# Transposing queries and keys on the DMA crossbar in place of TensorE, in an attention and MLP-mixer kernel

## The chip, the cores and the metric

The kernel runs on one core of one Trainium2 chip. The metric is the device time of one launch in microseconds (us); lower is better. A ratio is worked out from runs of both kernels in the same rounds on the same chip; it is not quite the ratio of the medians that are quoted beside it.

## The reference

Eight batches, eight heads, 576 tokens, head size 64. Block-causal attention (blocks of 64) is followed by an MLP mixer: a token mix with width 256 and a channel mix with width 1536, both with residuals.

```python
# q, k, v: (8, 8, 576, 64), drawn as randn * 0.1
scores = (1 / np.sqrt(64)) * q @ k.transpose(0, 1, 3, 2)
scores = np.where(block_i >= block_j, scores, -1e9)      # blocks of 64
attn = softmax(scores)
x = (attn @ v).transpose(0, 2, 1, 3).reshape(8, 576, 512)
h = relu(x.transpose(0, 2, 1) @ w_tok1) @ w_tok2         # 576 -> 256 -> 576
u = x + h.transpose(0, 2, 1)
out = u + relu(u @ w_ch1) @ w_ch2                        # 512 -> 1536 -> 512
```

## The kernel before

Heads are worked on in pairs, four pairs per batch, 32 in all (pair 0 to pair 31). GpSimd (POOL) issues the loads into SBUF, the on-chip memory, which also cast to bf16; queries and keys arrive there with tokens on the partitions (the 128 rows of that memory). The score matmul needs the head dimension on the partitions, so both must be transposed: five 128x128 blocks per tensor and pair, on TensorE into PSUM, the memory that its results go to, and copied from there. The keys of the two heads go into two tiles whose other half stays zero, so each score matmul spans all 128 partitions.

```python
def attention_pair(b, hp, x_sb, preloaded=None):
    qraw, kraw = preloaded if preloaded is not None else load_qk_pair(b, hp)

    qT_ps = ps_tr.tile([128, SP], BF16, name="trp")
    for c in range(NS):                                   # NS = 5, SP = 640
        nc.tensor.transpose(qT_ps[:, 128 * c : 128 * (c + 1)], qraw[:, c], ident)
    qT = qkT_p.tile([128, SP], BF16, name="qT")
    nc.vector.tensor_copy(qT, qT_ps)
    kT_ps = ...                                           # the same for kraw
    kTh = [r_kta.next(), r_ktb.next()]
    nc.vector.tensor_copy(kTh[0][0:64, :], kT_ps[0:64, :])
    nc.scalar.copy(kTh[1][64:128, :], kT_ps[64:128, :])

    for hh in range(2):
        # ... load v1; score matmuls into PSUM tiles sc[0..3]
        # ... ScalarE: exp(sc) -> e[0..3];  VectorE: four masks (memset) on e
        # ... value matmuls, into a free part of sc[3]
        nc.vector.reciprocal(rinv, u_view[:, :, 64:65])
        nc.vector.tensor_tensor(out=x_sb[...], in0=u_view[...], in1=rinv[...], op=MULT)
        # ... and a second tensor_tensor for the last 64 tokens
```

The pairs of batch b are traced between the parts of the mixer of batch b-1. A list scheduler then fixes each engine's instruction order when the program is built. At run time every engine works strictly in that order.

```python
for b in range(B + 1):
    attention_pair(b, 0, x_sb)
    pu_sb = token_mix(px)                  # of batch b-1, and so on
    p_uT = transpose_u(pu_sb)
    channel_gT(p_uT, p_gT, 0, 4)
    attention_pair(b, 1, x_sb)
    channel_gT(p_uT, p_gT, 4, 8)
    attention_pair(b, 2, x_sb)
    channel_gT(p_uT, p_gT, 8, 12)
    attention_pair(b, 3, x_sb)
    channel_h2_out(pb, p_gT, pu_sb)        # stores 1.15 MB on SP's DMA queue
```

The softmax here doesn't subtract the row's maximum and nothing guards it: scores larger than these inputs give would overflow.

## Time and profile before

| | before |
|---|---|
| median time | 415.43 us (2 runs, 415.31 to 415.54) |
| span in the profile | 412.9 us |
| first token-mix matmul of batch 1's mixer | 99.90 us |
| from one batch's first token-mix matmul to the next one's | 46.23 us, five times, then 45.67 |
| from the last of these boundaries (376.71) to the end | 36.2 us |

The first token-mix matmul of each batch is the clock that this document uses: its start times are read off the TensorE timeline. The mixer of batch 0 (its first one is at 41.38 us) runs beside pairs 4 to 7 and belongs to the start. From here on, "the first boundary" is that of batch 1's mixer, "a batch" is the stretch from one boundary to the next (the first of them holds pairs 8 to 11), and "a late batch" is one of the last of these.

Two lines of the page of before matter beyond those that the prediction shows: busy time by engine, and the queue that SP feeds (packets, MB, share of 16 engines). The third, from a table of stretches, is one exact batch (columns: length, busy time of PE, PEld, DVE, ACT, POOL with counts, granted clock, DMA share, GB/s).

```profile
PE 368.6 (89%) x3194; PEld 229.3 (56%) x3232; DVE 175.8 (43%) x674; ACT 221.4 (54%) x507; POOL 261.0 (63%) x403
...
q1 hardware_dynamic: 4864, 9.44, 6.3%
```

### The profile page before, as it was taken

To read this page: it belongs to the slowest core of one execution; us is meant where nothing else is said; L and a number is where in the kernel's file an instruction comes from. 1 tells how busy PE (TensorE), PEld (TensorE's weight loads), DVE (VectorE), ACT (ScalarE), POOL (GpSimd) and SP (SyncE) were. 2 spreads that over 40 slices of the span, in tenths; PEclk is the share of its full clock that TensorE was granted. 3 is DMA by queue.
4 is the path that set the end of the run, shared out by engine and by line. 5 is a ranking of instruction groups with operands and counts; after the bars stand their busy time and mean duration, and the time that the engine had idled before them with its cause. 6 is when DMAs were issued, how large, how long until landed. Compare 5 with 4: busy or idle time off the path is not lost.

```text
span 412.9 us, 8622 instructions
## 1 busy us (share of the span) xinstructions
PE 368.6 (89%) x3194; PEld 229.3 (56%) x3232; DVE 175.8 (43%) x674; ACT 221.4 (54%) x507; POOL 261.0 (63%) x403
## 2 busy tenths in 40 slices
PE   1676659999999999999999999999999999999996
PEld 1454247754676456744666457744666457744752
DVE  2244324543545364543554363543555363534112
ACT  9635037742677058742687058732687068730830
POOL 9999389999999775983679375973679320000000
PEclk9998859999999999999999999999999999999999
DMA  6999999999988894785668494885658550003003
GB/s 40 103 60 111 206 78 58 59 60 152 74 58 57 52 156 31 51 54 128 42 41 54 33 154 30 52 52 129 44 38 51 51 110 0 2 2 114 2 2 114
DMA packets 124730, 27.91 MB, mean 68 GB/s; under 512 B 117200, under 2 KB 119568, under 8 KB 124688
## 3 DMA queue, kind: packets, MB, share of 16 engines
q0 software_dynamic: 119824, 17.92, 60.2%
q1 hardware_dynamic: 4864, 9.44, 6.3%
q8 instruction: 26, 0.43, 0.4%
q14 instruction: 16, 0.13, 0.1%
HBM read 35.78 MB, written 9.44 MB: 110 GB/s over the span
## 4 chain that ended last, share of the span: by engine, by line
PE 52%; ACT 22%; POOL 9%; DVE 8%; DMA 5%; issue 3%; ACTq 0%; POOLq 0%
PE mps L336 22%; PE mps L319 18%; ACT e L224 6%; ACT e L223 5%; ACT kTb L195 5%; DMA wc_sb<-in_moe_w_ch_dram 4%; PE sc L238 4%; ACT e L225 3%; PE sc L214 3%; DVE u_sb L290 3%; POOL qraw L116 2%; POOL v L202 2%; ACT uT L306 2%; DVE qT L188 1%; ACT gT L326 1%
## 5 line engine op out<-in xcount | busy, mean ns | idle before, releaser
L319 PE MATMUL mps<-uT,wc_sb 128*128 128x288 bf16 x768 | 111.6, 286 | 1.0
L336 PE MATMUL mps<-wc_sb,gT 128*128 128x512 bf16 x464 | 110.8, 379 | 0.8
L319 PEld LDWEIGHTS <-wc_sb 128*128 128x128 bf16 x768 | 71.0, 97 | 28.4 <-issue 10.6
L116 POOL DMA_DIRECT2D qraw<-in_q_dram x64 | 55.3, 864 | 43.8 <-PE trp L192 28.8
L326 ACT ACTIVATE gT<-mps 128x288 bf16<-128x288 f32 x144 | 59.0, 410 | 28.1 <-PE mps L319 20.7
L336 PEld LDWEIGHTS <-gT 128*128 128x128 bf16 x480 | 44.5, 98 | 50.8 <-issue 5.1
L195 ACT COPY kTb<-trp 64x640 bf16<-64x640 bf16 x32 | 22.0, 687 | 89.5 <-DVE kTa L194 89.1
L202 POOL DMA_DIRECT2D v<-in_v_dram x64 | 56.3, 880 | 21.4 <-PE sc L214 18.5
L116 POOL DMA_DIRECT2D kraw<-in_k_dram x64 | 56.5, 883 | 7.0 <-PE trp L192 5.2
L343 DVE TENSOR_TENSOR o_sb<-mps,u_sb 128x512 f32<-128x512 f32 (+1 forms) x40 | 27.6, 690 | 71.3 <-PE mps L336 71.3
L238 PEld LDWEIGHTS <-e 128*128 128x128 bf16 x960 | 41.6, 101 | 16.9 <-issue 6.9
L214 PE MATMUL sc<-qT,kTb 128*128 128x64 bf16 (+4 forms) x190 | 43.7, 292 | 2.9 <-issue 0.4
L122 POOL DMA_DIRECT2D kraw<-in_k_dram x64 | 42.3, 660 | 1.0 <-DMA wc_sb<-in_moe_w_ch_dram 1.0
L122 POOL DMA_DIRECT2D qraw<-in_q_dram x64 | 40.9, 640 | 2.7 <-DMA wc_sb<-in_moe_w_ch_dram 2.7
L238 PE MATMUL sc<-v,e 128*128 128x65 bf16 x900 | 41.7, 195 | 1.1 <-ACT e L226 0.8
L206 POOL DMA_DIRECT2D v<-in_v_dram x64 | 41.4, 647 | 0.4 <-PE sc L214 0.3
L225 ACT ACTIVATE e<-sc 128x512 bf16<-128x512 f32 x60 | 36.0, 600 | 3.3 <-PE sc L214 1.5
L224 ACT ACTIVATE e<-sc 128x512 bf16<-128x512 f32 x60 | 35.7, 595 | 3.7 <-PE sc L214 3.7
L223 ACT ACTIVATE e<-sc 128x512 bf16<-128x512 f32 x60 | 35.8, 597 | 3.4 <-PE mps L238 1.9
L306 ACT COPY uT<-trp 128x512 bf16<-128x512 bf16 (+1 forms) x36 | 19.5, 544 | 29.9 <-PE trp L301 28.8
L326 DVE TENSOR_SCALAR gT<-mps 128x288 bf16<-128x288 f32 x48 | 22.0, 458 | 26.1 <-PE mps L319 25.6
L214 PE MATMUL sc<-qT,kTa 128*128 128x64 bf16 (+4 forms) x162 | 27.8, 280 | 4.3 <-ACT e L223 2.6
(61 smaller groups left out, 367.9 us busy)
## 6 DMA issues: line engine op xcount, KB each, us to landing
out_dram<-o_sb SPq DMA_DIRECT2D x8, 1024.0 KB, 4.3
qraw<-in_q_dram POOLq DMA_DIRECT2D x64, 64.0 KB, 2.8
kraw<-in_k_dram POOLq DMA_DIRECT2D x64, 64.0 KB, 2.7
v<-in_v_dram POOLq DMA_DIRECT2D x64, 64.0 KB, 2.8
wc_sb<-in_moe_w_ch_dram POOLq DMA_DIRECT2D x4, 384.0 KB, 6.8
wc_sb<-in_moe_w_ch_dram POOLq DMA_DIRECT2D x6, 256.0 KB, 11.9
qraw<-in_q_dram POOLq DMA_DIRECT2D x64, 8.0 KB, 2.3
kraw<-in_k_dram POOLq DMA_DIRECT2D x64, 8.0 KB, 2.3
```

What stands on the lines that cost most here:

```text
L116: nc.gpsimd.dma_start(out=t[:, c0:c1, hh, :], in_=src[b, 2 * hp + hh, 128 * c0 : 128 * c1, :].rearrange("(c p) d -> p c d", p=128),)
L122: nc.gpsimd.dma_start(out=t[0:64, 4, hh, :], in_=src[b, 2 * hp + hh, 512:576, :])
L195: nc.scalar.copy(kTh[1][64:128, :], kT_ps[64:128, :])
L202: nc.gpsimd.dma_start(out=v1[:, 0:4, 0:64], in_=v[b, h, 0:512, :].rearrange("(c p) d -> p c d", p=128),)
L214: nc.tensor.matmul(out=sc[tix][:, c0 : c0 + wdt], lhsT=kT[:, j0 : j0 + 128], rhs=qT[:, ist : ist + wdt], start=True, stop=True,)
L223: nc.scalar.activation(e[0], sc[0], EXP, scale=scale)
L224: nc.scalar.activation(e[1][:, 0:512], sc[1], EXP, scale=scale)
L225: nc.scalar.activation(e[2][:, 0:512], sc[2], EXP, scale=scale)
L238: nc.tensor.matmul(out=u_view[:, I, 0:65], lhsT=exp_lhsT(e, I, J), rhs=v1[:, J, 0:65], start=(J == 0), stop=(J == I),)
L319: nc.tensor.matmul(out=g_ps[:, 0:288], lhsT=wc1_sb[:, m, 128 * cc : 128 * (cc + 1)], rhs=uT[:, m, 288 * sh : 288 * (sh + 1)], start=(m == ...
L326: nc.any.tensor_scalar_max(gT[:, cc, 288 * sh : 288 * (sh + 1)], g_ps[:, 0:288], 0.0)
L336: nc.tensor.matmul(out=h2_ps, lhsT=gT[:, cc, 128 * si : 128 * (si + 1)], rhs=wc2_sb[:, cc, :], start=(cc == 0), stop=(cc == NDC - 1),)
```

## The change

The intent is to take the transposes of queries and keys off TensorE, the bound. The DMA crossbar does them from SBUF to SBUF, one instruction per tensor and pair, issued from SP. The query copy and the PSUM tiles go with them; both key copies move to VectorE.

```diff
-        qT_ps = ps_tr.tile([128, SP], BF16, name="trp")
-        for c in range(NS):
-            nc.tensor.transpose(qT_ps[:, 128 * c : 128 * (c + 1)], qraw[:, c], ident)
-        qT = qkT_p.tile([128, SP], BF16, name="qT")
-        nc.vector.tensor_copy(qT, qT_ps)
-        (the same for kT_ps, from kraw)
+        qT = qkT_p.tile([128, NS, 128], BF16, name="qT")
+        nc.sync.dma_start_transpose(
+            out=qT, in_=qraw.rearrange("p c h d -> p (c h d)")
+        )
+        qT = qT.rearrange("p c s -> p (c s)")
+        (the same for kTr, from kraw)
         kTh = [r_kta.next(), r_ktb.next()]
-        nc.vector.tensor_copy(kTh[0][0:64, :], kT_ps[0:64, :])
-        nc.scalar.copy(kTh[1][64:128, :], kT_ps[64:128, :])
+        nc.vector.tensor_copy(kTh[0][0:64, :], kTr[0:64, :])
+        nc.vector.tensor_copy(kTh[1][64:128, :], kTr[64:128, :])
```

More of the change, by code (lines that the diff above doesn't have):

```diff
@@ L182, in attention_pair @@
         qraw, kraw = preloaded if preloaded is not None else load_qk_pair(b, hp)
-        qT_ps = ps_tr.tile([128, SP], BF16, name="trp")
-        for c in range(NS):
-            nc.tensor.transpose(qT_ps[:, 128 * c : 128 * (c + 1)], qraw[:, c], ident)
-        qT = qkT_p.tile([128, SP], BF16, name="qT")
-        nc.vector.tensor_copy(qT, qT_ps)
-        kT_ps = ps_tr.tile([128, SP], BF16, name="trp")
-        for c in range(NS):
-            nc.tensor.transpose(kT_ps[:, 128 * c : 128 * (c + 1)], kraw[:, c], ident)
+        qT = qkT_p.tile([128, NS, 128], BF16, name="qT")
[3 more added lines that the diff above has]
+        qT = qT.rearrange("p c s -> p (c s)")
+        kTr = qkT_p.tile([128, NS, 128], BF16, name="kTr")
+        nc.sync.dma_start_transpose(
+            out=kTr, in_=kraw.rearrange("p c h d -> p (c h d)")
+        )
+        kTr = kTr.rearrange("p c s -> p (c s)")
         kTh = [r_kta.next(), r_ktb.next()]
-        nc.vector.tensor_copy(kTh[0][0:64, :], kT_ps[0:64, :])
-        nc.scalar.copy(kTh[1][64:128, :], kT_ps[64:128, :])
+        nc.vector.tensor_copy(kTh[0][0:64, :], kTr[0:64, :])
+        nc.vector.tensor_copy(kTh[1][64:128, :], kTr[64:128, :])
         for hh in range(2):
```

## The prediction

> **What bounds the kernel now.** I read the page's 40 slices first, then a table of stretches, one per batch, then the TensorE timeline at a batch boundary, and last the waits. The slices:
>
> ```profile
> PE   1676659999999999999999999999999999999996
> PEclk9998859999999999999999999999999999999999
> DMA  6999999999988894785668494885658550003003
> ```
>
> TensorE (PE) is full from slice 7 on, at full granted clock; before that it is not, while DMA is. So there are two regimes. The stretches (columns: length, busy time and instruction count of PE, PEld, DVE, ACT, POOL, then granted clock, DMA share, GB/s):
>
> ```profile
> 0.00:53.30 53.30, 29.58 (x225) 17.52 (x228) 17.07 (x92) 25.98 (x68) 44.63 (x74) 0.93 0.99 106
> 53.30:99.50 46.20, 42.50 (x385) 27.79 (x388) 18.97 (x78) 24.37 (x55) 45.57 (x71) 0.90 0.92 62
> 192.00:238.20 46.20, 44.24 (x403) 27.59 (x406) 21.98 (x82) 26.33 (x59) 31.52 (x48) 1.00 0.69 65
> 330.70:376.90 46.20, 44.23 (x400) 27.50 (x402) 21.96 (x82) 26.33 (x59) 2.65 (x4) 1.00 0.13 30
> ```
>
> A steady batch takes 46.2 us, with PE busy 44.2, ACT 26.3, DVE 22.0. In the last of them DMA has nearly stopped (0.13) and the period is the same: data movement doesn't set it, TensorE does. In the first two stretches POOL, which issues all loads, is busy 44.6 and 45.6 us: the start is paced by load issue. What the change removes stands in the timeline at a batch boundary (start, length, engine, line, operation):
>
> ```profile
> 145.57 0.44 PE L186 MATMUL trp<-ident,qraw 128*128 128x128 bf16 x5
> 145.85 0.44 PE L192 MATMUL trp<-ident,kraw 128*128 128x128 bf16 x5
> 146.13 1.24 PE L266 MATMUL mps<-x_sb,w_sb 128*128 128x512 bf16 x4
> ```
>
> The next group starts 0.28 us after each group of five: a pair of tensors really occupies 0.56 us of TensorE, not 10 x 219 ns. The waits tell where loads hold TensorE (us, times, longest), and how long the ring makes the loads wait for the transposes:
>
> ```profile
> PE trp L186 <- DMA qraw<-in_q_dram: 13.5, 3, 6.8
> PEld L186 <- DMA qraw<-in_q_dram: 7.2, 1, 7.2
> PE trp L192 <- DMA kraw<-in_k_dram: 5.0, 7, 1.9
> POOL qraw L116 <- PE trp L192: 28.8, 8, 8.4
> ```
>
> The first three all fall before about 62 us; later the loads are ahead and wait for room.
>
> **What the Trainium skill says.** (1) "VectorE: DVE Perf Modes", The three transpose paths: 390 ns for a 128x128 bf16 transpose on TensorE, 1309 ns on the DMA crossbar. Our trace has 219 ns for one record and 56 ns as spacing in a run of five, so the page's figure is that of one alone; I take 56. (2) "DMA: Bandwidth & Descriptors", Latency and other measured facts: an effective 261 GB/s for the DMA transpose in one kernel, 350 to 400 when contiguous. One instruction here moves 128 x 640 x 2 B = 164 KB, an estimate of 0.63 us at 261 GB/s. (1) read literally for five blocks in a row gives 6.5 us. The two differ tenfold, and no transpose is in the trace of before; this is the main uncertainty. (3) The same page, DMA Transpose (X-bar) and SWDGE vs HWDGE vs iDMA: this transpose is issued from SP or ACT only, and its descriptors are generated in hardware. So it doesn't lengthen POOL's issue queue, and SP has little else: in the waits it sat 384.6 us waiting for output tiles. (4) "SBUF — State Buffer", SBUF: two separate sides: a fast VectorE copy within SBUF and GpSimd's descriptor writing lock each other out. The new key copies are of that kind; before, their source was PSUM. Each lasts well under a POOL issue (0.77 us), so I give it at most 1 us in the whole kernel.
>
> **The change part by part.**
> TensorE loses 64 groups of five transposes: 64 x 0.28 = 17.9 us. Not all of it counts. Pairs 0 to 3 run before 53 us, where TensorE waits for loads anyway: 0. Pairs 4 to 7 (the stretch 53.3 to 99.5) are still paced by POOL, at 1.3 us per load and its tail, six loads per pair, 7.8 us per pair, against score groups 7.6 us apart in the chain: I count 0.5 us of their 2.24. Batches 2 to 7 (pairs 8 to 31) are TensorE's: 24 x 0.56 = 13.4 us. Sum: 13.9 us.
> VectorE loses the query copy (486 ns) and the PSUM form of the key copy (476 ns) and gains two 64x640 copies from SBUF. The trace has no such copy; I guess 0.25 us each. Net -0.46 us of 5.5 us per pair: off the path. ScalarE loses 687 ns per pair. That copy stands on the chain with 4.5% of the span, but the chain follows releasers: in steady batches TensorE had work from the mixer meanwhile. The direct TensorE waits there sum to 1.2 us per batch, 0.2 of them for scores behind the exponential. I count nothing.
> The crossbar gains 64 instructions, 8 per batch: 8 x 0.63 = 5 us of 46.2. The DMA share of 0.69 then becomes 0.80. I take issue to landing as 3.3 us, an estimate: in this trace a 128 KB output store lands in 2.9 us, plus some queueing. In steady state that is hidden. The query buffer of pair p is free after the scores of pair p-4, loads are at least two pairs ahead (20 us), and a transpose needs neither the PE order nor the PSUM slots.
> At the start it is not hidden. Pair 2's scores began at 28.07 and pair 3's at 35.50, just after their keys had landed; each comes some 3 us later. The stall before pair 4 absorbs that, 6.78 us of TensorE idle before 55.23. In the changed instruction order the transposes of u and 22 channel matmuls (2.7 us) stand ahead of pair 4's scores, so TensorE works there while the crossbar does; then pairs 5 to 7 are again load plus 3.3 us. I count +1.5 us for the start.
> Moved work: comparing instruction orders, the scheduler brings the second pair of a batch forward into the token-mix section, where before there was one pair. In that section ScalarE must do four heads of exponentials (4 x 1.65 = 6.6 us, at 0.5 us spacing), one ReLU 0.6 and four uT copies 2.4: 9.6 us, against some 10 us of TensorE work (scores 2.7, values 1.9, token mix 4.3, transposes 1.2). That is nearly a tie, in order on both sides, so I charge 0.4 us per batch of extra stalls: 6 x 0.4 = 2.4 us.
> Sum: 415.4 - 13.9 + 1.5 + 2.4 = 405.4. Greedy scheduling may equally fill holes that existed (about 2 us of idle PE per batch), so I shade it down a little: 404 us.
>
> **The rivals.**
> The crossbar is slow. At 6.5 us per instruction the SP queue needs 8 x 6.5 = 52 us per batch, above 46.2: it becomes the bound, and the kernel goes to 64 x 6.5 = 419 plus about 40 of start and tail, some 455 us. For it: the page's 1309 ns, and small DMA packets here are slow (119824 packets take 60.2% of 16 engines for 412.9 us, 33 ns each). Against it: the 261 GB/s, and at 33 ns each the 640 rows of 256 B cost only 640 x 33 / 16 = 1.3 us. In between, at 2 to 3 us, a batch needs 16 to 24 us beside about 32 us of present DMA time: a near tie, 410 to 425 us. I give 12% to clearly slow and 10% to the middle.
> The gain is eaten by waits. The crowded section becomes ScalarE's, or VectorE, in order, stalls at a key copy whose transpose is late and holds back the masks and normalisation behind it. Then the period stays near 46 and the time is 410 to 416 us. For it: ACT 9.6 against PE 10. Against: ACT is busy only 26.3 of 46.2 us over a batch, and the DVE copies come long after the transposes.
> The full gain. Nothing is lost at the boundary and the start is neutral: 415.4 - 13.9, less about 3 us of holes filled, 398 us.
>
> **Range and chances.** The 2% line is 407.1 us. Between the full gain (398) and gain eaten (415) I see 404 as middle, with the line inside the spread, and a tail above it from a slow crossbar. Low 397, high 424. Faster by over 2%: 0.57; within: 0.27; slower: 0.16.
>
> **What would show it.** Right: no trp from qraw or kraw; steady stretches of about 44.2 us; crossbar landings near 3 us and a DMA share near 0.8; TensorE rows without waits on VectorE's key copies after 100 us. Wrong in the crossbar: landings of 6 us and more, DMA share near 1 in every stretch, VectorE waiting for transposes in steady batches, the period above 48. Wrong in the boundary: the same landings, but PE idle behind ACT between the token mix and the first channel matmuls, period at 46. Wrong in the start: the first batch's end moves by more than 3 us from 99.5.

## More of the kernel before

```profile
284.82:331.04 46.22, 44.25 (x402) 27.63 (x405) 21.97 (x83) 26.33 (x59) 31.52 (x48) 1.00 0.69 65
```

TensorE is busy 44.25 of 46.22 us, so 1.97 us per batch are idle. SP's queue carries the output stores only.

## The result, and the profile after

The changed kernel takes 410.19 us (median of 2 runs, 409.72 to 410.66). The ratio to before is 0.988, 95% interval 0.984 to 0.992: some 1.2% faster, less than half of what was predicted. Its profile has a span of 408.9 us.

The slices of the page after:

```profile
PE   0254079999749689999999999999999999999996
...
PEclk9966559999959899999999999999999999999999
DMA  7999999999999999989999999778629341003003
```

The same four stretches as in the prediction, then, in the fifth and sixth row, two exact batches (columns as above):

```profile
0.00:53.30 53.30, 14.33 (x130) 9.01 (x132) 10.41 (x72) 19.69 (x57) 43.41 (x71) 0.76 1.12 116
53.30:99.50 46.20, 42.75 (x379) 26.41 (x381) 23.40 (x96) 25.68 (x63) 43.89 (x67) 0.91 1.24 108
192.00:238.20 46.20, 45.59 (x393) 27.85 (x396) 22.73 (x89) 25.21 (x61) 45.41 (x70) 1.00 1.25 117
330.70:376.90 46.20, 45.28 (x377) 27.42 (x381) 19.14 (x75) 24.72 (x59) 2.62 (x4) 1.00 0.19 51
104.76:162.98 58.22, 45.66 (x363) 27.78 (x366) 22.37 (x85) 24.29 (x59) 55.21 (x85) 0.88 1.23 113
289.45:331.47 42.02, 41.57 (x362) 25.85 (x365) 19.62 (x80) 24.11 (x59) 10.54 (x16) 1.00 0.53 59
```

(The DMA share adds up the times of all packets. It can pass 1, as in four of these rows, when packets of one engine overlap.) Two things contradict each other at first sight. Late in the kernel a batch takes 42.02 us, 4.2 us less than before, with TensorE busy 41.57. But one batch, 104.76 to 162.98, takes 58.22 us, for nearly the same number of matmuls. The start suffered too: in the first 53 us TensorE is busy 14.33 us, where it was 29.58. The start times of the first token-mix matmuls give the whole account:

| stretch | before, us | after, us | difference |
|---|---|---|---|
| start to first boundary | 99.90 | 104.76 | +4.9 |
| first batch after it | 46.23 | 58.22 | +12.0 |
| next five batches, sum | 230.58 | 209.73 | -20.9 |
| last boundary to end | 36.2 | 36.2 | 0.0 |
| span | 412.9 | 408.9 | -4.0 |

The TensorE timeline at a late boundary (start, length, engine, line, operation) has no transposes of queries or keys any more, and scores stand between the token-mix matmuls:

```profile
288.80 0.82 PE L215 MATMUL sc<-qT,kTa 128*128 128x512 bf16 x5
289.45 0.38 PE L267 MATMUL mps<-x_sb,w_sb 128*128 128x512 bf16 x1
289.86 0.19 PE L215 MATMUL sc<-qT,kTa 128*128 128x64 bf16 x1
290.10 0.38 PE L267 MATMUL mps<-x_sb,w_sb 128*128 128x512 bf16 x1
```

The waits after (engine, tile and line, what it waited for: us, times, longest):

```profile
DVE kTa L195 <- DMA kTr<-kraw: 53.4, 11, 11.4
...
PE mps L215 <- DVE kTa L195: 37.1, 4, 13.6
...
PE sc L215 <- DVE x_sb L255: 7.5, 1, 7.5
...
PE sc L239 <- DVE e L231: 3.2, 1, 3.2
```

VectorE (DVE) now waits 53.4 us for transposed keys, in only 11 places. TensorE waits 37.1 us for key copies in the start (L215 with `mps`, the first batch's even heads), and 7.5 us once for VectorE's normalisation of `x_sb`. That last wait is in the long batch, and the two timelines around it show what happened. VectorE first:

```profile
107.75 0.21 DVE L255 TENSOR_TENSOR x_sb<-sc,rinv 64x64 bf16<-64x64 f32 x1
108.02 0.09 DVE L233 MEMSET e<- 64x32 uint32 x1
108.06 0.09 DVE L234 MEMSET e<- 64x32 uint32 x1
115.83 0.32 DVE L195 COPY kTa<-kTr 64x640 bf16<-64x640 bf16 x1 [7.68 <-DMA kTr<-kraw]
116.07 0.18 DVE L248 RECIPROCAL rinv<-sc 128x5 f32<-128x5 f32 x1
...
116.94 0.42 DVE L249 TENSOR_TENSOR x_sb<-sc,rinv 128x256 bf16<-128x256 f32 x1
117.28 0.20 DVE L255 TENSOR_TENSOR x_sb<-sc,rinv 64x64 bf16<-64x64 f32 x1
```

and TensorE in the same time:

```profile
109.44 0.60 PE L215 MATMUL sc<-qT,kTa 128*128 128x512 bf16 x3
117.54 0.66 PE L215 MATMUL sc<-qT,kTa 128*128 128x320 bf16 x3 [7.51 <-DVE x_sb L255]
```

VectorE stands 7.68 us at a key copy (L195) whose transpose hasn't landed. Behind that copy, in VectorE's order, stands the normalisation of another pair (pair 8, second head), whose value matmuls TensorE had finished at about 108.7. It reads `sc`, and TensorE's next scores, of pair 9, need that PSUM buffer. So TensorE stops too, for 7.51 us. The keys at which VectorE waited belong to pair 10, whose own scores are far from due (they begin at 133.52); nothing but the order made them urgent. The 3.2 us wait in the list above is a second stall of the kind, in the same batch: VectorE stood 5.93 us at the keys of pair 13, until 137.85, with masks for TensorE's next value matmuls behind them. SP's timeline shows when the transpose of pair 10's keys was issued:

```profile
104.98 1.20 SPq L185 DMA_TRANSPOSE qT<-qraw  x1
106.69 0.41 SPq L347 DMA_DIRECT2D out_dram<-o_sb  x1
107.23 0.56 SPq L351 DMA_DIRECT2D out_dram<-o_sb  x1
108.18 3.00 SPq L190 DMA_TRANSPOSE kTr<-kraw  x1
```

It was issued 1 us behind the output store of batch 0, and it landed 7.6 us after its issue, about twice the median. But it couldn't have been issued much earlier: the last load of these keys had landed at 108.03. VectorE came to the copy at 108.15 (115.83 less 7.68), before the transpose was even issued, so a landing of the usual length would have stopped it as well, for less long. The queue and issue lines give that median (last column):

```profile
q1 hardware_dynamic: 47872, 19.93, 24.5%
...
qT<-qraw SPq DMA_TRANSPOSE x32, 3.8
kTr<-kraw SPq DMA_TRANSPOSE x32, 3.6
```

The crossbar's share of the queue is 24.5% less the stores' 6.3% of before, 18.2% of 16 engines' 408.9 us: 74.4 us, or 1.16 us of packet time per transpose (an estimate, as the stores are taken to cost what they did before).

### The profile page after: what moved, and what is told of

The parts are those of the page before. It is cut to its first block, busy times and chain, and to the rows that moved or that the text cites. A ratio compares the mean times of both kernels' runs of the same rounds, so it can differ in the third digit from the quotient of the medians.

```text
span 408.9 us, 8119 instructions
## 1 busy us (share of the span) xinstructions
PE 346.4 (85%) x2881; PEld 212.9 (52%) x2912; DVE 162.4 (40%) x653; ACT 203.3 (50%) x496; POOL 262.0 (64%) x403
## 3 DMA queue, kind: packets, MB, share of 16 engines
q1 hardware_dynamic: 47872, 19.93, 24.5%
## 4 chain that ended last, share of the span: by engine, by line
PE 73%; DMA 12%; POOL 6%; issue 3%; DVE 3%; ACT 2%; POOLq 0%; ACTq 0%; SPq 0%; DVEq 0%
PE mps L337 24%; PE mps L320 21%; PE sc L215 10%; PE sc L239 7%; DMA kTr<-kraw 6%; DMA v<-in_v_dram 5%; PE mps L267 4%; PE mps L284 4%; PE trp L302 2%; POOL kraw L116 1%; POOL qraw L116 1%; DMA kraw<-in_k_dram 1%; POOL kraw L122 1%; POOL qraw L122 1%; ACT e L224 1%
## 5 line engine op out<-in xcount | busy, mean ns | idle before, releaser
L320 PE MATMUL mps<-uT,wc_sb 128*128 128x288 bf16 x768 | 108.0, 287 | 0.4
L203 POOL DMA_DIRECT2D v<-in_v_dram x64 | 58.6, 916 | 46.1 <-PE sc L215 33.2
L327 ACT ACTIVATE gT<-mps 128x288 bf16<-128x288 f32 x167 | 68.4, 411 | 23.4 <-PE mps L320 12.8
L116 POOL DMA_DIRECT2D qraw<-in_q_dram x64 | 61.5, 968 | 17.1 <-DMA qT<-qraw 7.6
L116 POOL DMA_DIRECT2D kraw<-in_k_dram x64 | 62.4, 978 | 4.3 <-issue 2.5
L122 POOL DMA_DIRECT2D kraw<-in_k_dram x64 | 47.1, 736 | 2.0 <-DMA wc_sb<-in_moe_w_ch_dram 1.1
L215 PEld LDWEIGHTS <-kTa 128*128 128x128 bf16 x192 | 16.7, 102 | 59.4 <-DVE kTa L195 25.3
L122 POOL DMA_DIRECT2D qraw<-in_q_dram x64 | 46.6, 727 | 1.6 <-DMA wc_sb<-in_moe_w_ch_dram 1.6
L207 POOL DMA_DIRECT2D v<-in_v_dram x64 | 43.4, 678 | 1.6 <-DMA w_sb<-in_moe_w_tok_dram 1.6
L215 PE MATMUL sc<-qT,kTb 128*128 128x64 bf16 (+3 forms) x191 | 43.3, 294 | 0.6 <-DMA kraw<-in_k_dram 0.2
L215 PE MATMUL mps<-qT,kTa 128*128 128x64 bf16 (+4 forms) x24 | 6.6, 416 | 37.1 <-DVE kTa L195 37.1
L215 PE MATMUL sc<-qT,kTa 128*128 128x512 bf16 (+1 forms) x168 | 28.5, 279 | 9.0 <-DVE x_sb L255 7.5
L195 DVE COPY kTa<-kTr 64x640 bf16<-64x640 bf16 x32 | 12.3, 385 | 56.8 <-DMA kTr<-kraw 53.4
```

The costliest lines, as they stand in the source:

```text
L116: nc.gpsimd.dma_start(out=t[:, c0:c1, hh, :], in_=src[b, 2 * hp + hh, 128 * c0 : 128 * c1, :].rearrange("(c p) d -> p c d", p=128),)
L122: nc.gpsimd.dma_start(out=t[0:64, 4, hh, :], in_=src[b, 2 * hp + hh, 512:576, :])
L203: nc.gpsimd.dma_start(out=v1[:, 0:4, 0:64], in_=v[b, h, 0:512, :].rearrange("(c p) d -> p c d", p=128),)
L207: nc.gpsimd.dma_start(out=v1[0:64, 4, 0:64], in_=v[b, h, 512:576, :])
L215: nc.tensor.matmul(out=sc[tix][:, c0 : c0 + wdt], lhsT=kT[:, j0 : j0 + 128], rhs=qT[:, ist : ist + wdt], start=True, stop=True,)
L320: nc.tensor.matmul(out=g_ps[:, 0:288], lhsT=wc1_sb[:, m, 128 * cc : 128 * (cc + 1)], rhs=uT[:, m, 288 * sh : 288 * (sh + 1)], start=(m == ...
```

## The experiments

Twelve kernels ran, eleven of them to explain the time. Ratios are to the kernel before in the same rounds (its medians there: 414.41, 414.99 and 414.63 us).

**No transposes at all** (a wrong result):

```diff
-        (the two crossbar transposes and the two key copies)
+        qT = r_qt.next()                       # fixed tiles, set to zero once
+        kTh = [r_kta.next(), r_ktb.next()]
```

> No transposes at all: queries and keys are fixed zero tiles, the result is wrong on purpose; loads, exponentials and the rest stay. This is what the change could win at most. Theory A (the changed kernel loses its gain in the loaded first 160 us, to keys that land late): steady batches of 42 us as in the changed kernel, a start as in the kernel before, so 415.4 - 6 x 4.2 - 1 = about 389 us. Rival (the 42 us of the changed kernel come from data being further ahead, not from TensorE's work): steady batches of 44 us, about 401 us.

Measured: 401.87 us, ratio 0.969 (0.967 to 0.971). It isn't the clean bound that it was meant to be: nothing reads the loaded queries and keys any more, so the loads come in another order and the values come late. TensorE's waits:

```profile
PE sc L227 <- DMA v<-in_v_dram: 25.7, 11, 10.5
```

One batch, 177.25 to 235.02, takes 57.8 us. So the total is near the rival's 401 us by accident, as late batches aren't at its 44 us. What can be used is the late batch: 41.9 us (280.73 to 322.62), 0.1 less than with the crossbar. The crossbar doesn't hold up a late batch. A side finding: this kernel passes the correctness check. With inputs of 0.1 the attention is nearly uniform, and zero queries move the output by 1.0% in the norm (worked out on the reference). So that check says nothing about the transposes, which is why the last run below was made.

**The crossbar's work added to the kernel before, its result unread:**

```diff
+        for raw in (qraw, kraw):
+            unread = qkT_p.tile([128, NS, 128], BF16, name="unread")
+            nc.sync.dma_start_transpose(
+                out=unread, in_=raw.rearrange("p c h d -> p (c h d)")
+            )
         qT_ps = ps_tr.tile([128, SP], BF16, name="trp")
```

> The kernel before, with the 64 crossbar transposes added into tiles that nobody reads. Theory B (the crossbar's bytes take DMA capacity from the loads, which come late themselves): the first 160 us grow by 5 us or more, time 421 to 430 us. Theory A (only the late keys and what stands behind them cost): loads lag by little, time 415 to 418 us.

Measured: 416.83 us, ratio 1.006 (1.004 to 1.007). The boundaries stand at 102.39, 148.62, 194.85, 241.08: a batch still takes 46.23 us, and the loss, 2.5 us, lies ahead of the first boundary. A stretch as long as a batch:

```profile
240.00:286.24 46.24, 44.84 (x406) 27.64 (x404) 21.97 (x82) 26.33 (x59) 31.53 (x48) 1.00 0.86 94
```

The DMA share is 0.86, where the kernel before had 0.69 in its stretch of 192 to 238 us. So 64 crossbar transposes as a load on the DMA engines cost some 2.5 us in all, which may be up to half of the start's 4.9 us. The theory that the added DMA work itself ate the gain falls. Most of what hurts must be waiting for the result.

**No key copies** (the score matmuls read 64 partitions of the transposed keys directly):

```diff
-        kTh = [r_kta.next(), r_ktb.next()]
-        nc.vector.tensor_copy(kTh[0][0:64, :], kTr[0:64, :])
-        nc.vector.tensor_copy(kTh[1][64:128, :], kTr[64:128, :])
...
-                    lhsT=kT[:, j0 : j0 + 128],
-                    rhs=qT[:, ist : ist + wdt],
+                    lhsT=kTr[64 * hh : 64 * hh + 64, j0 : j0 + 128],
+                    rhs=qT[64 * hh : 64 * hh + 64, ist : ist + wdt],
```

> The changed kernel without the two VectorE key copies: the score matmuls take 64 partitions of the transposed tile directly. Theory A with VectorE's order as the carrier (a copy that waits for a late key holds up the normalisations behind it, 7.5 and 3.2 us of TensorE waits): these waits vanish, time 396 to 401 us; the wait for pair 3's keys behind the weights stays. Theory B: the same first 160 us, time 408 to 411 us.

Measured: 404.34 us, ratio 0.976 (0.972 to 0.980), above what was expected. The long batch is gone: the boundaries stand at 104.57, 148.44, 192.31 and so on. With no copy in VectorE's order there is nothing to wait at. But every batch now takes 43.87 us, not 42.0:

```profile
280.06:323.93 43.87, 43.87 (x365) 24.71 (x365) 17.05 (x72) 24.58 (x59) 10.56 (x16) 1.00 0.54 76
```

In that row TensorE is busy for the whole batch, and the change to its matmuls is that the scores read 64 partitions. Their records are no longer than before (387 ns for 512 columns, against 379 in the changed kernel), but the matmuls stand further apart where scores and others alternate: from the start of a 512-column score to that of another kind of matmul it is 319 ns, against 215 in the changed kernel (medians of 16, in late batches), while from such a score to the next score it is 227 against 216. Why, no run shows. The late copy as carrier is supported, but not alone, as the matmuls changed too.

**TensorE transposes for batches 0 to 2, the crossbar from batch 3:**

```diff
+        if b < 3:
+            (TensorE's transposes and copies, as before)
+        else:
+            (the crossbar)
```

> TensorE transposes as before for batches 0 to 2, the crossbar from batch 3 on. Both theories: the first 146 us as in the kernel before, then five batches at 42.1 instead of 46.2 us: 415.4 - 5 x 4.1 = about 395 us. If the steady gain needs the crossbar's early lead, more: 400 or above.

Measured: 413.53 us, ratio 0.997 (0.995 to 0.999): a plain miss. The start is as good as before (first boundary 99.61), but the next batch takes 66.8 us. The stall had moved to the first crossbar keys, those of pair 12:

```profile
121.57 0.32 DVE L209 COPY kTa<-kTr 64x640 bf16<-64x640 bf16 x1 [12.39 <-DMA kTr<-kraw]
```

That transpose was issued at 118.25 and landed in 3.3 us; VectorE had stood at the copy since 109.2. I had taken the stall for an effect of the crowded early DMA, gone after batch 2. Here it comes from a copy that the order puts far ahead of its transpose, with a quite usual landing: even the loads of these keys were issued only from 113.85 on, when VectorE had stood for 4.7 us.

**The key copies held back in VectorE's order**, behind the last normalisation of the previous pair's first head. An edge of order only, no wait is added:

```diff
+        with tc.issue_after(norms[-1][0]) if norms else ExitStack():
             nc.vector.tensor_copy(kTh[0][0:64, :], kTr[0:64, :])
             nc.vector.tensor_copy(kTh[1][64:128, :], kTr[64:128, :])
+        norms.append([])
...
+            norms[-1].append(last.ins)     # the second tensor_tensor into x_sb
```

> The changed kernel with one thing pinned: on VectorE, the two key copies of a pair are issued no earlier than the first head's normalisation of the pair before it (an issue order only, no wait). TensorE's own order in the steady batches is that of the changed kernel, instruction for instruction. Theory A (VectorE waits in order for keys that nobody needs yet): the batch of 58.4 us falls to 42 to 44, time 394 to 397 us. Rival (the keys are late for TensorE itself, as the order draws pairs forward): TensorE waits for the same keys instead, 407 us or more.

Measured: 399.73 us, ratio 0.962 (0.959 to 0.966). TensorE's order in a late batch is the same as in the changed kernel, instruction by instruction. The total is above the expected 394 to 397, since one later batch takes 47.21 us (TensorE waits 3.59 us for values there). The long batch is gone, in the band expected for it:

```profile
104.48:147.52 43.04, 41.74 (x362) 25.83 (x365) 20.46 (x79) 24.35 (x60) 39.70 (x62) 1.00 1.20 119
```

and VectorE's timeline around the same event is the cleanest evidence:

```profile
109.16 0.20 DVE L252 RECIPROCAL rinv<-sc 128x5 f32<-128x5 f32 x1
109.38 0.42 DVE L253 TENSOR_TENSOR x_sb<-sc,rinv 128x256 bf16<-128x256 f32 x1
109.72 0.21 DVE L259 TENSOR_TENSOR x_sb<-sc,rinv 64x64 bf16<-64x64 f32 x1
...
115.96 0.21 DVE L259 TENSOR_TENSOR x_sb<-sc,rinv 64x64 bf16<-64x64 f32 x1
...
116.75 0.59 DVE L198 COPY kTa<-kTr 64x640 bf16<-64x640 bf16 x1 [0.40 <-DMA kTr<-kraw]
```

The keys of pair 10 were again issued just behind batch 0's store (at 109.00) and again landed late (at about 116.7). But the normalisation that stood at 116.07 in the changed kernel now runs at 109.16, ahead of the copy. The copy still waits, 0.40 us, and TensorE doesn't. The transpose was as late as before, and 15.2 us of the batch are gone (58.22 to 43.04): the order carried the stall, and the late landing alone costs almost nothing.

**The same, behind the second head's normalisation** (`norms[-1][1]`):

> As the run before it, but behind the second head's normalisation: copies are later still and the second pair of a batch is no longer drawn so far forward. Theory A: the 58 us batch is gone too; if drawing the pair forward is what brings a steady batch from 44 to 42 us, steady batches are 43 to 44 us here and the time is 400 to 404; if not, 42 us and 394 to 397.

Measured: 400.83 us, ratio 0.967 (0.963 to 0.971), late batches 42.6 us, between the two bands expected; part of the second pair's scores and values stand later in TensorE's order than in the run before. For the long batch the exact place isn't critical: it takes 42.6 us too.

**The first of these two, and TensorE's transposes for batch 0:**

```diff
+        if b == 0:
+            (TensorE's transposes and copies, as before)
+        else:
+            (the crossbar, key copies held back)
```

> The pinned order, and TensorE transposes for batch 0, whose keys came 12 us late behind the channel weights. If these late keys are what moved the end of the first mixed batch from 99.9 to 104.1 us, this wins another 4 us on the pinned run: 390 to 393 us. Rival (the start is bound by load issue anyway): the same as the pinned run.

Measured: 392.62 us, ratio 0.947 (0.945 to 0.950), as expected, and the fastest version. The first boundary is at 100.93 in place of 104.48. The profiled spans of the two versions are 8.1 us apart: 3.6 of that is the first boundary, and 4.6 one later batch that had waited for values (47.21 us there, 42.64 here); that this second part comes from the edit isn't shown. The batch after the first boundary, with the DMA as full as ever:

```profile
100.93:142.88 41.95, 41.52 (x363) 25.86 (x365) 19.25 (x79) 24.33 (x60) 40.57 (x63) 1.00 1.29 122
```

**Stores issued from ScalarE's queue**, to ask whether the store ahead in SP's queue makes the transposes late:

```diff
-        nc.sync.dma_start(
+        nc.scalar.dma_start(
             out=out[b, 0:512, :].rearrange("(c p) d -> p c d", p=128),
```

> The changed kernel with the output stores issued from ScalarE's queue. The keys that landed 7.7 us after issue had been issued 1 us behind a 1.15 MB store on the same queue. If standing behind the store is what delays them: landing near 4 us, the 58 us batch shrinks by some 4 us, time 404 to 407. If the shared DMA engines delay them whatever the queue: 409 to 411.

Measured: 418.13 us, ratio 1.007 (1.004 to 1.009): missed, and inconclusive. ScalarE, in order as well, now waits for output tiles ahead of its exponentials:

```profile
ACT e L224 <- DVE o_sb L344: 77.6, 6, 13.1
```

VectorE still waits 55.5 us for keys, and the longest landing is 7.6 us. Pair 10's queries, issued at 106.33 while the stores from ScalarE's queue were under way (105.58 to 112.96), took 7.1 us: one case that points to the full DMA, and not enough to decide. So whether the store in the queue or the full DMA makes the late landing stays open. But the keys of pair 10, whose last load landed at 111.34, were issued at 111.96 and landed in a usual 3.6 us, and VectorE stood 8.68 us at their copy all the same, TensorE 6.84 us, in a batch of 59.4 us: the stall doesn't need a late landing. It repeated the lesson on another engine: an instruction that waits for something late holds back everything behind it.

**Where the other 1.9 us of a late batch come from.** A late batch is 4.2 us shorter, and TensorE's transposes are only 2.24 of it. Three kernels ask whether the rest comes from drawing the batch's second pair forward into the token mix. The first is the fastest version with one more edge of order on TensorE: the second pair's scores stand behind the transposes of u, as they did before.

```diff
+                with tc.issue_after(gate[0]) if gate and hp == 1 else ExitStack():
                     nc.tensor.matmul(out=sc[tix][:, c0 : c0 + wdt], ...)
...
+        gate[:] = [last.ins]               # the last transpose of u
         return uT
```

> Open: steady batches of the changed kernel are 4.1 us shorter than before, TensorE's transposes are only 2.24 of that. This is the fastest version so far (VectorE order pinned, TensorE transposes in batch 0) with one edge more: in TensorE's order the second pair's scores stand behind the transposes of u, as in the kernel before, not drawn forward into the token mix. Theory F (drawing the second pair forward fills holes and is worth the other 1.9 us): steady batches of 43.6 to 44.2 us, total 402 to 406. Theory W (the other 1.9 us are the waits of the chain transpose, copy from PSUM, scores, which are gone wherever the second pair stands): steady batches stay at 42.0 to 42.4, total 391 to 394.

Measured: 401.54 us, ratio 0.968 (0.967 to 0.970). Batches of 43.6 to 44.1 us, as the theory of the second pair (F) has it:

```profile
276.78:320.38 43.60, 42.24 (x367) 25.82 (x366) 19.73 (x80) 23.95 (x59) 10.57 (x16) 1.00 0.46 69
```

From 46.22 to 43.60 is 2.6 us, the transposes and 0.4; from 43.60 to 42.02 is 1.6 us, the second pair's place. Compared with the changed kernel's row, the gate's TensorE is busy 0.7 us longer and idle 0.9 us longer.

The second sends only the keys over the crossbar, with the copies held back, and leaves the queries on TensorE:

```diff
+        (TensorE's transposes of qraw and the copy to qT, as before)
-        qT = ...; nc.sync.dma_start_transpose(out=qT, ...)
         (keys: crossbar, copies held back)
```

> Half the dose: the keys go over the crossbar (copies pinned in VectorE's order), the queries stay on TensorE in all batches, so TensorE keeps 5 of 10 transposes per pair, 1.12 us per batch; the queries' PSUM slots also keep the second pair behind the transposes of u. Theory F: steady batches 46.2 - 1.1 = 45.1 us. Theory W: half or more of the whole 4.1 us, as the query copy still hangs on the chain but the keys don't: 43.5 to 44.2 us. Crossbar time per batch is halved, so landings should be shorter too; total 400 to 408.

Measured: 409.84 us, ratio 0.987 (0.985 to 0.990), just above the total expected. One of its batches:

```profile
283.07:327.59 44.52, 43.46 (x388) 26.97 (x385) 21.82 (x85) 23.75 (x57) 21.04 (x32) 1.00 0.56 66
```

44.52 us lies between the two theories' bands: 1.7 us gained where half the transposes are 1.12. The second pair wasn't drawn forward here either.

The third is the kernel before with the second pair traced ahead of the token mix:

```diff
         attention_pair(b, 0, x_sb)
+        attention_pair(b, 1, x_sb)
         (token mix, transposes of u, channel matmuls 0 to 3)
-        attention_pair(b, 1, x_sb)
```

> The kernel before, all transposes on TensorE, with the second pair of a batch traced ahead of the token mix, so that its scores and values interleave with it. Theory F: steady batches fall from 46.2 by up to 1.9 us, to 44.3 to 45.0, total 402 to 408. Theory W: steady batches within 0.5 us of 46.2, total 411 to 419.

Measured: 415.82 us, ratio 1.003 (1.000 to 1.005), batches of 45.83 us. Drawing forward alone is worth 0.4 us, not 1.6. So it pays together with the crossbar only; with TensorE's transposes and their copies in the same stretch it doesn't. Which of those takes the benefit away, the runs don't separate. Nor do they tell why half the transposes gave 1.7 us.

**Are the transposes right?** Both are made, and 1000 times their difference is added to the queries:

```diff
+        for x, ref in ((xb[0], qT), (xb[1], kT_ps)):     # xb: from the crossbar
+            nc.vector.tensor_tensor(out=d, in0=x, in1=ref, op=subtract)
+            nc.vector.tensor_scalar_mul(dm, d, 1000.0)
+            nc.vector.tensor_tensor(out=qn, in0=qT, in1=dm, op=ADD)
+            qT = qn
```

> Not about time. The correctness check passes even with all queries and keys zero (the first run of the study), so it doesn't show that the crossbar transposes are right. Here both are made: TensorE's transposes are used as before, and 1000 times the difference (crossbar minus TensorE), of queries and of keys, is added to the transposed queries. If the crossbar delivers the same bits, the difference is zero everywhere and the output stays correct. If even one block of 128 rows of one pair differs, the output must fail: worked out on the reference, adding 1000 times the difference of two such blocks to one block of one head changes the whole output by 74% in the norm, against 1.0% for zero queries. Time expected 430 to 460 us, as VectorE does six more large operations per pair.

Measured: correct, in one run (425.39 us, below the range that I had given for the time). So the crossbar's blocks equal TensorE's in all pairs, as far as a check can see that counts their difference a thousandfold.

## Why the prediction was wrong

The direction and the bound were right, and so was the main term: without the transposes a late batch is shorter. The predicted 404.0 us and the measured 410.19 differ because two of its steps failed in one direction, and a third, failing in the other, hid part of it. (Its sum was 405.4, shaded to 404.) That the total falls into the second rival's 410 to 416 us is luck: the period didn't stay near 46, it was 42 with one batch of 58.

| step | predicted, us | measured, us |
|---|---|---|
| start, with pairs 4 to 7 | +1.5 - 0.5 = +1.0 | +4.9 |
| each batch after it | -2.24 + 0.4 = -1.84 | five times -4.2 |
| six batches, sum | -11.0 | -20.9 and once +12.0 |

**The step that failed most is the second rival's, and there the words "the DVE copies come long after the transposes".** The prediction had named the mechanism: VectorE, in order, stalls at a late key copy and holds back what stands behind it. It set it aside because the copies were late on average. But a wait is set by one copy, not by the average: in the built order a copy for pair 10 stood ahead of the normalisation of pair 8, VectorE stood at it from 108.15 on, just as its transpose was issued (108.18), and the landing took 7.6 us. That batch costs 58.22 - 42.02 = 16.2 us more than a late one. The held-back copies show that it is the order: with the transpose as late, the batch takes 43.04. The built order was there to be read before the prediction; what was missing was the question which waiting instruction stands ahead of which urgent one.

Not all of the 16.2 us is idle time. TensorE is idle 58.22 - 45.66 = 12.6 us in the long batch against 0.45 in a late one; the other 4.1 us are longer busy time, at a granted clock of 0.88. The Trainium skill, "TensorE: Matmul & The Clock Gate", Part 1: The HAM clock gate, says that an idle window of some 3.4 us puts TensorE's clock down to half until it has been busy as long again. The trace agrees in kind: the batch with gaps of 7.51 and 3.24 us has 0.88 (half rate is recorded from 112.60 to 122.84 and from 139.90 to 143.32), the same batch without them (copies held back) 1.00.

**The start was mis-sized**: +1.5 us for a landing of 3.3 us. The median landing is near that, 3.6 us for keys, but in the start the longest is 11.9 us: pair 3's keys, issued at 39.44 while the loads of the channel weights were being issued (38.0 to 45.7), landed at 51.4. The four first scores waited 37.1 us for key copies. That the first boundary moved by more than 3 us was the prediction's own sign for this. With TensorE's transposes in batch 0 the first boundary is back at 100.93.

**The boundary had the wrong sign.** The prediction charged 0.4 us per batch for the second pair being drawn forward. With the crossbar it is worth -1.6 us (the gate run); ScalarE at 24.1 of 42.0 us didn't become the bound. With the transposes' own 2.6 us in place of 2.24, that is the 4.2.

**The crossbar's size was off and didn't matter.** 1.16 us of packet time against 0.63 assumed; the per-packet estimate of 1.3, given as an argument only, was nearer. The DMA share became 1.25 in the third stretch, not 0.80, and the period in that stretch was still near 42; part of the 1.25 is that more loads fall into the stretch (70 instructions on POOL, 48 before). The unread transposes cost 2.5 us in all. VectorE's key copies took 308 to 739 ns against 250 assumed; it is their place in the order that mattered, not their length. Whether the longer ones waited for GpSimd, as the prediction's point (4) would have it, no run tests. (A slip without effect: 64 x 6.5 is 416, not 419.)

Still open: what makes single landings two to three times the median, and which part of TensorE's transposes spoils the drawn-forward order.

## What to carry to other kernels

When work moves from an engine to a DMA, ask which instructions now wait for that DMA and what stands behind them in the same engine's order: one late landing stalls everything behind it, though its own result isn't due. Holding such copies back, behind the work that frees buffers for the bound engine, gave some 2.6% here (ratio 0.962 after 0.988), and the version that also leaves the first batch on the old path another 1.6% (0.947), under half of it in the start. And check that the correctness check can see the change: here zero queries passed.

## What the Trainium skill lacked or had wrong

- "VectorE: DVE Perf Modes", The three transpose paths: its 1309 ns for one 128x128 block on the crossbar can't be scaled by blocks. Here one instruction with five blocks (128x640 in bf16) took 1.20 us to issue on SP, 1.16 us of the 16 DMA engines and 3.6 to 3.8 us from issue to landing (median), not 6.5 us.
- "DMA: Bandwidth & Descriptors", Latency and other measured facts: its 261 GB/s wasn't seen. 164 KB in 1.16 us of packet time is 141 GB/s, an estimate beside the loads of this kernel, whose packets share the engines, with 672 packets per transpose. It gives no spread of the landing, which was 2.6 to 11.9 us for keys.
- "PSUM — Partial Sum Buffer", Engine vs sequencer instructions: it says that VectorE's queue is strictly first in, first out, and the trace agrees (a normalisation that was ready at about 108.7 ran at 116.07, behind a waiting copy). It lacks what that means for a DMA's late result: a copy that isn't due yet holds back the work that frees PSUM for TensorE; the batch with two such stalls took 16.2 us more here.
